# Loading the second weight matrix later, and accumulating the second matmul of the first two blocks and of the last quarter in one PSUM bank

## The chip, the cores and the metric

The kernel runs on one core of a Trainium2 chip. The metric is the device time of one execution in microseconds (us). Executions of the same kernel mostly spread over about 1 to 4 us here, so a difference of one microsecond needs several runs of both kernels on the same chip. Next to times I use profiles: one recorded execution per kernel, whose absolute times are exact for that execution but carry that execution's luck.

Engines are called as in the profile: PE is TensorE's matmuls and PEld its weight loads, DVE is VectorE, ACT is ScalarE, POOL is GpSimd, SP is SyncE. A "q" behind a name (POOLq) is the engine's instruction queue, which issues DMAs.

## The reference

```python
def _attn_ref(x, weight_gen):            # x (8, 4096, 192), weight_gen (8, 4096, 8, 7)
    w = softmax(weight_gen, axis=-1)     # 7 taps for each token and head
    # causal convolution over 7 tokens with these weights, 24 channels a head
    return einsum('bshk,bskhg->bshg', w, x_unf)   # ... unfolding cut

def _moe_ref(x, w_in, w_out):            # w_in (192, 2048), w_out (2048, 192)
    h = np.maximum(x @ w_in, 0.0)
    return h * h @ w_out
```

So 32,768 tokens go through a softmax, a convolution with weights that differ by token, and a feed-forward layer with a squared ReLU.

## The kernel before

All matmuls are in 16-bit floats. The tokens are worked off in blocks: two of 512 tokens, then 31 of 1024 (I call the first one block 0). For each block the softmax of the gate weights (`ex`, `ssum`, `rcp`, `v_first` or `v_big`) is written to bands: rows of it are read by DMA into `wr`, and VectorE multiplies them with a mask into band matrices `bd`. TensorE then does three kinds of matmul: the convolution (`yp`, line 393), the first matmul of the feed-forward layer (`h`, line 418) and the second (`o`, line 450). Between the last two, ScalarE evicts `h` with a ReLU into `t` and VectorE squares it into `g`.

The second matmul of a block is done during the next block, in passes (`M` in the schedule strings) of eight 128-row chunks and two 128-token columns. Before the change, each chunk is split into two 64-row halves that accumulate into two PSUM banks; ScalarE copies the first and VectorE adds the second:

```python
    def new_o(pool, tag):
        if pool is ps_o:
            return [ps_o.tile([P, TB], f32, name=f"o{i}") for i in range(2)]
        o = pool.tile([P, 2, TB], f32, name="o", tag=tag)
        return [o[:, 0], o[:, 1]]

    def st_mm2(j, qt, fcs, ccs, o):
        # ... half, off, per: cut
        for fc in fcs:
            g = g_t[(j, fc // per)][:, half, fc % per * th + off :]
            for cc in ccs:
                for oo, r0 in zip(o, (0, RT)):
                    nc.tensor.matmul(
                        out=oo[:, cc * Dm : (cc + 1) * Dm],
                        lhsT=g[r0 : r0 + RT, cc * P : (cc + 1) * P],
                        rhs=w_o[r0 : r0 + RT, fc, :],
                        start=(fc == 0 and cc == ccs[0]), stop=(fc == NF - 1),
                        skip_group_check=True,
                        tile_position=(r0, 0),
                    )

    def o_sum(j, qt, ccs, o):
        # ... cut
        nc.scalar.copy(out=o_sb, in_=o[0][:, c])
        nc.vector.tensor_tensor(out=o_sb, in0=o[1][:, c], in1=o_sb, op=AluOp.add)
```

The pool `ps_o` has one buffer for each of the two banks, so the next output's first matmul of a bank waits until that bank has been read: for the second bank, until VectorE's add.

The start of the kernel, which the change touches too, in the order in which the loads are issued:

```python
        spin(42)
        band_mask()
        s0.load(nc.sync)
        # ... w_in first half, first x, w_in second half, first softmax: cut
        x_load_f32(1)
        nc.scalar.copy(out=w_i[:, 1, 0], in_=w_st[1])
        cross_w_in(1)
        s1.load(nc.sync)
        # ... bands and convolution of block 0: cut
        x_cast(1, nc.vector.tensor_copy)

        nc.gpsimd.memset(x_t[0][:, 0, 0:1], 0.0)
        for q in (0, 1):
            load_w_out(q, 4)
        nc.gpsimd.memset(x_st[1][:, 0:1], 0.0)
        for q in (2, 3):
            load_w_out(q, 4)
        s2.load(nc.gpsimd)
        nc.gpsimd.memset(v_big, 0.0)
```

`s0`, `s1` and `s2` are the first three softmax parts; `s1.load` fetches the gate weights of the second. `spin(42)` is a warm-up of TensorE with matmuls on zeros. A `memset` on one element of a tile that something else still reads is a gate: GpSimd has to wait for that reader before it can go on to issue the loads behind it.

The softmax here doesn't subtract the row's maximum and nothing guards it: scores larger than these inputs give would overflow.

## Time and profile before

| | before |
|---|---|
| median of 3 runs | 753.37 us (753.17 to 754.48) |
| profiled span | 751.2 us |
| TensorE busy | 737.4 us, 98% |
| TensorE waits, 12 to 66 us | 8.0 us |
| after the last matmul | 3.66 us |

How to read this: an engine that is busy 98% of the span can only be helped where it is not busy. Busy shares of the other engines (VectorE and ScalarE 83% each) say that they can be the bound for a stretch, not overall. The lines that carry this stand in the prediction.

### The profile page before, as it was taken

What the parts mean: (1) busy time and instruction counts of PE and PEld (TensorE: products, weight loads), DVE (VectorE), ACT (ScalarE), POOL (GpSimd) and SP (SyncE); (2) the same over time, 40 slices, a digit from 0 to 9 for tenths busy, and PEclk for the clock granted to TensorE, in tenths of its full rate; (3) what the DMA queues carried; (4) which work ended last, traced back from release to release, by engine and by line L of the source; (5) the groups of instructions that cost most, each with busy time, mean ns of one, the idle gap of its engine ahead of it and who ended that gap; (6) DMA issues with size and microseconds to landing.
All of it is one profiled execution on the core that took longest, in us unless ns stands there. A gap on an engine that the chain in (4) does not pass through costs nothing.

```text
span 751.2 us, 33616 instructions
## 1 busy us (share of the span) xinstructions
PE 737.4 (98%) x15266; PEld 562.8 (75%) x15266; DVE 624.4 (83%) x1007; ACT 623.3 (83%) x753; POOL 88.0 (12%) x128
## 2 busy tenths in 40 slices
PE   8799999999999999999999999999999999999998
PEld 4667777777777787777877777787778777777787
DVE  5799999899789888888888888898888987777853
ACT  5787898888888888888888888888888888888883
POOL 4522221011101010011000110001100011001000
PEclk9999999999999999999999999999999999999999
DMA  8746443546443444533345442365341454441312
GB/s 222 130 80 126 68 76 91 114 94 139 72 87 97 85 79 79 116 92 63 57 80 139 82 81 51 55 138 107 59 73 51 59 108 79 59 74 50 50 45 65
DMA packets 122330, 65.22 MB, mean 87 GB/s; under 512 B 83881, under 2 KB 118668, under 8 KB 121676
## 3 DMA queue, kind: packets, MB, share of 16 engines
q1 hardware_dynamic: 77868, 46.05, 22.3%
q0 software_dynamic: 44176, 16.93, 20.4%
q8 instruction: 119, 1.95, 1.0%
q14 instruction: 23, 0.19, 0.1%
q10 hardware_dynamic: 144, 0.10, 0.0%
HBM read 48.61 MB, written 28.70 MB: 103 GB/s over the span
## 4 chain that ended last, share of the span: by engine, by line
PE 91%; DVE 4%; DMA 2%; SPq 1%; issue 1%; ACT 0%; POOL 0%; DVEq 0%; ACTq 0%
PE o L450 44%; PE h L418 42%; PE yp L393 6%; DVE g L430 1%; DMA wg<-in_weight_gen_dram 1%; DMA wr<-v_first 1%; DVE v_first L216 1%; DVE bd L325 1%; SPq L307 0%; DVE ssum L201 0%; DVE rcp L208 0%; SPq L125 0%; POOL wr L307 0%; DVE o_sb L465 0%; ACT ex L194 0%
## 5 line engine op out<-in xcount | busy, mean ns | idle before, releaser
L427 ACT ACTIVATE t<-h 128x1024 f16<-128x1024 f32 x512 | 497.2, 1027 | 66.0 <-PE h L418 64.9
L430 DVE TENSOR_TENSOR g<-t 128x1024 f16<-128x1024 f16 x512 | 334.4, 688 | 99.3 <-ACT t L427 96.3
L450 PEld LDWEIGHTS <-g 64*128 64x128 f16 x8192 | 351.7, 94 | 56.5 <-issue 3.7
L450 PE MATMUL o<-w_o,g 64*128 64x192 f16 x8192 | 384.0, 243 | 2.9 <-DVE o_sb L465 1.8
L418 PE MATMUL h<-y,w_i 64*128 64x512 f16 (+1 forms) x3168 | 377.7, 370 | 4.2 <-DMA w_i<-w_i 1.5
L418 PEld LDWEIGHTS <-w_i 64*128 64x128 f16 x3168 | 167.0, 94 | 112.9 <-issue 4.8
L325 DVE TENSOR_TENSOR bd<-wr,mask 128x4160 f16<-128x4160 f16 (+3 forms) x89 | 149.5, 1703 | 5.6 <-DMA wr<-v_first 5.6
L277 POOL DMA_DIRECT2D xt<-in_x_dram x62 | 51.3, 832 | 443.3 <-PE yp L393 420.4
L464 ACT COPY o_sb<-o 128x384 f32<-128x384 f32 x129 | 62.2, 482 | 34.0 <-PE o L450 34.0
L465 DVE TENSOR_TENSOR o_sb<-o,o_sb 128x384 f32<-128x384 f32 x129 | 71.2, 552 | 10.1 <-ACT o_sb L464 7.6
L404 ACT CAST y<-yp 128x1024 f16<-128x1024 f32 (+1 forms) x64 | 48.1, 802 | 16.4 <-PE yp L393 16.4
L393 PE MATMUL yp<-bd,xt 128*32 128x104 f16 (+8 forms) x3864 | 52.1, 208 | 1.8 <-DVE bd L325 1.6
L393 PEld LDWEIGHTS <-xt 128*32 128x32 f16 (+3 forms) x3864 | 46.2, 91 | 8.0 <-issue 7.4
L194 ACT ACTIVATE ex<-wg 128x448 f32<-128x448 f32 (+2 forms) x44 | 27.2, 619 | 3.6 <-DMA wg<-in_weight_gen_dram 3.6
L216 DVE TENSOR_TENSOR v_big<-ex,rcp 128x112 f16<-128x112 f32 (+1 forms) x136 | 27.4, 264 | 2.5 <-DMA vd<-v_big 1.3
L201 DVE TENSOR_REDUCE ssum<-ex 128x64 f32<-128x448 f32 (+2 forms) x44 | 26.1, 594 | 2.4 <-ACT ex L194 2.4
L208 DVE RECIPROCAL rcp<-ssum 128x64 f32<-128x64 f32 (+2 forms) x44 | 23.7, 539 | 1.5
L267 POOL DMA_DIRECT2D xt<-in_x_dram x7 | 3.8, 549 | 137.1 <-PE yp L393 137.1
L307 POOL DMA_DIRECT2D wr<-v_first x31 | 16.8, 562 | 21.3 <-DVE v_first L216 21.1
L512 PE MATMUL wp<-warm 128*128 128x512 f16 x42 | 10.8, 423 | 1.3 <-DVE warm L504 1.3
L512 PEld LDWEIGHTS <-warm 128*128 128x128 f16 x42 | 4.4, 108 | 7.1 <-issue 2.1
L216 DVE TENSOR_TENSOR v_first<-ex,rcp 128x112 f16<-128x112 f32 (+1 forms) x48 | 9.1, 256 | 0.3
(20 smaller groups left out, 24.6 us busy)
## 6 DMA issues: line engine op xcount, KB each, us to landing
out_dram<-o_sb SPq DMA_DIRECT2D x63, 384.0 KB, 2.9
xt<-in_x_dram POOLq DMA_DIRECT2D x42, 240.0 KB, 5.9
wg<-in_weight_gen_dram SPq DMA_DIRECT2D x4, 1064.0 KB, 8.4
xt<-in_x_dram POOLq DMA_DIRECT2D x20, 192.0 KB, 5.6
wr<-vd SPq DMA_DIRECT2D x38, 80.0 KB, 5.1
vd<-v_big SPq DMA_DIRECT2D x5, 512.0 KB, 5.6
wg<-in_weight_gen_dram SPq DMA_DIRECT2D x5, 392.0 KB, 5.2
wg<-in_weight_gen_dram SPq DMA_DIRECT2D x3, 616.0 KB, 5.8
```

Of the source, the lines that this page charges most:

```text
L194: nc.scalar.activation(out=self.ex[:, lo:hi].rearrange("p r g k e -> p (r g) k e"), in_=self.wg[:, lo:hi].rearrange("p r (g e) k -> p (r g ...
L216: eng.tensor_tensor(out=bass.AP(tensor=v.tensor, offset=v.offset + lo * H * SL + lo % SL * 2 + g * SL * 2, ap=[list(v.ap[0]), [H * SL + 2, ...
L277: eng.dma_start(out=dst[:, first:last], in_=ap)
L325: nc.vector.tensor_tensor(out=bd_t[j][:, H * lo : H * (lo + len(tiles) * n)].rearrange("p (g m c) -> p g m c", g=shape[1], c=2 * SL), in0= ...
L393: nc.tensor.matmul(out=yps[k // per][p0 : p0 + m, col + a : col + b], lhsT=x_t[s][:, i, 32 * q : 32 * q + m], rhs=bd[:, h // 2, h % 2, a - ...
L404: nc.scalar.copy(out=y[:, k0:k1, 0:th], in_=yp[:, 0 : (k1 - k0) * th].rearrange("p (k c) -> p k c", c=th),)
L418: nc.tensor.matmul(out=h[:, half, jj * th : (jj + 1) * th], lhsT=w_in_chunk(u * per + jj, slot, half), rhs=y_t[j][r0 : r0 + RT, k, 0:th], ...
L427: nc.scalar.activation(out=t1, in_=h, func=ActF.Relu)
L430: nc.vector.tensor_tensor(out=g, in0=t1, in1=t1, op=AluOp.mult)
L450: nc.tensor.matmul(out=oo[:, cc * Dm : (cc + 1) * Dm], lhsT=g[r0 : r0 + RT, cc * P : (cc + 1) * P], rhs=w_o[r0 : r0 + RT, fc, :], start=(f ...
L464: nc.scalar.copy(out=o_sb, in_=o[0][:, c])
L465: nc.vector.tensor_tensor(out=o_sb, in0=o[1][:, c], in1=o_sb, op=AluOp.add)
```

## The change

The intent has three parts. First, all of `w_out` is loaded behind the cast of the second x, so that the first half of it no longer shares the DMA engines with the second x, the second half of `w_in` and the gate weights of the second softmax. Second, in the first two blocks the second matmul uses all 128 rows of the array and one bank: no VectorE add and no wait for a second bank. Third, the last quarter of the last block does the same, so that the final store does not wait for an add. The diff, without blank-line hunks:

```diff
@@ -431,11 +432,11 @@
 
     QT = 2 * P
 
-    def new_o(pool, tag):
+    def new_o(pool, banks=2):
         if pool is ps_o:
-            return [ps_o.tile([P, TB], f32, name=f"o{i}") for i in range(2)]
-        o = pool.tile([P, 2, TB], f32, name="o", tag=tag)
-        return [o[:, 0], o[:, 1]]
+            return [ps_o.tile([P, TB], f32, name=f"o{i}") for i in range(banks)]
+        o = pool.tile([P, 2, TB], f32, name="o", tag="h")
+        return [o[:, i] for i in range(banks)]
 
     def st_mm2(j, qt, fcs, ccs, o):
 
@@ -446,11 +447,13 @@
         for fc in fcs:
             g = g_t[(j, fc // per)][:, half, fc % per * th + off :]
             for cc in ccs:
-                for oo, r0 in zip(o, (0, RT)):
+                n = P // len(o)
+                for i, oo in enumerate(o):
+                    r0 = n * i
                     nc.tensor.matmul(
                         out=oo[:, cc * Dm : (cc + 1) * Dm],
-                        lhsT=g[r0 : r0 + RT, cc * P : (cc + 1) * P],
-                        rhs=w_o[r0 : r0 + RT, fc, :],
+                        lhsT=g[r0 : r0 + n, cc * P : (cc + 1) * P],
+                        rhs=w_o[r0 : r0 + n, fc, :],
                         start=(fc == 0 and cc == ccs[0]), stop=(fc == NF - 1),
                         skip_group_check=True,
                         tile_position=(r0, 0),
@@ -462,7 +465,8 @@
         c = slice(ccs[0] * Dm, (ccs[-1] + 1) * Dm)
         o_sb = o_sb_t[(j, qt // 2)][:, qt % 2, c]
         nc.scalar.copy(out=o_sb, in_=o[0][:, c])
-        nc.vector.tensor_tensor(out=o_sb, in0=o[1][:, c], in1=o_sb, op=AluOp.add)
+        if len(o) == 2:
+            nc.vector.tensor_tensor(out=o_sb, in0=o[1][:, c], in1=o_sb, op=AluOp.add)
 
     def o_store(j, qt, chunks, eng):
 
@@ -543,11 +547,8 @@
         st_bands(1)
         x_cast(1, nc.vector.tensor_copy)
 
-        nc.gpsimd.memset(x_t[0][:, 0, 0:1], 0.0)
-        for q in (0, 1):
-            load_w_out(q, 4)
         nc.gpsimd.memset(x_st[1][:, 0:1], 0.0)
-        for q in (2, 3):
+        for q in range(4):
             load_w_out(q, 4)
         s2.load(nc.gpsimd)
         nc.gpsimd.memset(v_big, 0.0)
@@ -656,7 +657,7 @@
                     qt, part = divmod(m, 2)
                     m += 1
                     if part == 0:
-                        o = new_o(ps_o, None)
+                        o = new_o(ps_o, 1 if j < 3 else 2)
                     st_mm2(j - 1, qt, FCS[part], (0, 1), o)
                     if part == 1:
                         o_sum(j - 1, qt, (0, 1), o)
@@ -679,7 +680,7 @@
         j = NBLK - 1
         nq = 2 * BLOCKS[j][1]
         for qt in range(nq - 1):
-            o = new_o(ps_o if qt % 2 else ps_h, "h")
+            o = new_o(ps_o if qt % 2 else ps_h)
             st_mm2(j, qt, range(NF), (0, 1), o)
             o_sum(j, qt, (0, 1), o)
             if qt % 2:
@@ -687,7 +688,7 @@
             elif qt == nq - 2:
                 o_store(j, qt, (0, 1), nc.sync)
         for cc, eng in ((0, nc.sync), (1, nc.scalar)):
-            o = new_o((ps_h, ps_o)[cc], "h")
+            o = new_o((ps_h, ps_o)[cc], 1)
             st_mm2(j, nq - 1, range(NF), (cc,), o)
             o_sum(j, nq - 1, (cc,), o)
             o_store(j, nq - 2, (2 + cc,), eng)
```

New line numbers are 1 to 4 higher in the changed kernel: the convolution is L394, the first matmul L419, the second L453, the copy L467, the add L469, the exponential L195, the band product L326.

## The prediction

> **What bounds the kernel now.** I read the busy shares first, then the waits of the matmul engine by stretch of time, then the chain of waits and the timeline of the first 66 us, because the busy shares average stages with different limits.
>
> ```profile
> PE 737.4 (98%) x15266; PEld 562.8 (75%) x15266; DVE 624.4 (83%) x1007; ACT 623.3 (83%) x753; POOL 88.0 (12%) x128
> ```
>
> TensorE is busy for 98% of 751.2 us. Grouped by line between 62 and 747 us, its three kinds of matmul have together 0.1 us of idle time before them:
>
> ```profile
> L450 PE MATMUL o<-w_o,g 64*128 64x192 f16 x7909 | 370.0, 243 | 0.1
> L418 PE MATMUL h<-y,w_i 64*128 64x512 f16 x2880 | 353.6, 376 | 0.0
> L393 PE MATMUL yp<-bd,xt 128*32 128x104 f16 (+3 forms) x3480 | 45.9, 208 | 0.0
> ```
>
> So from 62 us on the time is pure TensorE work, and the change leaves that stretch alone until the last quarter. It can only win (a) TensorE idle time before 62 us, (b) what comes after the last matmul (747.6 us), and it can lose (c) if it makes a matmul pass dearer. The waits of TensorE from 12 to 66 us show what there is to win in (a): 8.2 us in six groups.
>
> ```profile
> PE o L450 <- DVE o_sb L465: 1.8, 2, 1.2
> PE yp L393 <- DVE bd L325: 1.6, 3, 1.1
> PE h L418 <- DMA w_i<-w_i: 1.5, 1, 1.5
> PE h L418 <- ACT t L427: 1.4, 2, 1.1
> PE h L418 <- ACT y L404: 0.9, 1, 0.9
> PE o L450 <- DVE g L430: 0.8, 1, 0.8
> ```
>
> Columns: who waited for whom, us in total, times, longest. The first row is the PSUM bank that VectorE has not yet added up; the third is the copy of w_in between partition halves that landed late; the others are mostly echoes of a late softmax. The chain of waits shows why it is late (start, us, what):
>
> ```profile
> 14.31 7.19 DMA wg<-in_weight_gen_dram
> ...
> 40.41 0.47 DVE o_sb L465
> ...
> 60.58 0.48 DVE o_sb L465
> ...
> 61.10 1.48 PE o L450 x31
> ```
>
> The gate weights of the second softmax take 7.19 us to land, at 21.50; those of the first took 3.18 us. ScalarE stands still for them (timeline, idle before in brackets):
>
> ```profile
> 21.60 0.94 ACT L194 ACTIVATE ex<-wg 128x784 f32<-128x784 f32 x1 [1.66 <-DMA wg<-in_weight_gen_dram]
> ```
>
> Everything up to 61 us hangs behind that exponential, through VectorE (sum, reciprocal, scaling, band products, squares). The DMA queues between 16.5 and 20.5 us say who is in the way:
>
> ```profile
> q0 software_dynamic: 917, 0.34, 74.8%
> q1 hardware_dynamic: 277, 0.64, 48.4%
> ```
>
> Columns: packets, MB, share of 16 engines (both together pass 100% because packets overlap). q0 here is nothing but the first quarters of w_out, issued from GpSimd at 13.43 and 14.21; q1 carries the second x, the second w_in copy and the gate weights. 0.34 MB of small packets take more engine time than 0.64 MB of what the engines are waiting for.
>
> **What the Trainium skill says.** "Trainium Kernel Development and Optimization", Key Constraints: DMAs of all queues run on the same 16 engines and interleave; the two shares above agree. "TensorE: Matmul & The Clock Gate", "Wait — 56ns, not 53.3ns?": a warm matmul of N columns costs N/2.4 + 2.5 ns, so 82.5 ns for 192 columns. The trace agrees for pairs of 64-row halves: a pass of 32 (16 pairs) takes 1.32 us of the chain, 82.5 ns a pair. The same page, "Back-to-back issue gap", gives 81 ns for a sustained weight-load-and-matmul of 128 columns, which I take as a hint that a weight load hides behind 80 ns of matmul but barely; no whole-array matmul of 192 columns stands in this trace (the warm-up's 512-column ones run at about 213 ns, weight loads hidden). "TensorEngine Tiling (Array Packing)", Key Properties: changing the tiling mode drains TensorE. The trace fits: from the last second-matmul start (57.03) to the first convolution matmul (57.20) is 0.17 us against 0.08 for a pair, so about 0.1 us a switch.
>
> **Part 1, w_out moved.** Nothing is removed; two of four loads (0.2 MB each as written) go behind the cast of the second x. From 16.5 to 21 us q1 moved about 0.67 MB at 48% of the engines or less. At the rate it had alone just before (about 0.17 MB per 0.5 us at 15.5), that is 2 us, so x lands near 17.1 instead of 17.7, the w_in copy near 18.0 instead of 19.99, and the gate weights near 18.9 instead of 21.50. The four w_out loads then are issued from about 17.9 at 0.75 us each; with about 2 us to the first packet they start near 19.8, after the gate weights.
> The gain is not 2.6 us, because ScalarE is busy with four first-matmul evictions until 19.95: the exponential moves from 21.60 to about 19.85, that is 1.75 us. TensorE's 1.48 us wait for the w_in copy (18.55 to 20.04) disappears too, but it is the same time: its next unit then waits for ScalarE behind that exponential. VectorE's sum and scaling, and the reads of the band rows, follow 1.75 us earlier.
> Does w_out come in time? First use moves from 24.84 to about 23.1, the second eight chunks from 26.8 to about 25.1. At 1.1 us a quarter (landings of the last two before: 22.87 and 23.89) I get 21.2, 22.3, 23.4, 24.4: in time by about 1 us each, and TensorE waits there for VectorE's squares anyway (0.76).
>
> **Part 2, one bank for blocks 0 and 1.** It removes four VectorE adds of 0.55 us, and the wait for the second bank. Two of the adds (at 30.34 and 47.50) stand before a wait for band rows (1.30 and 0.76 idle) and are worth nothing. The add at 40.33 is on the chain: 0.46. So VectorE is then 1.75 + 0.46 = 2.2 us early up to the squares that end at 60.58. The add at 60.49 is on the chain with the wait it causes: TensorE stood still 1.16 us before 61.10. The bank copied by ScalarE is free at 59.37, so this goes. Of it I give back 0.4: two passes later TensorE needs the square that VectorE does behind the softmax piece (at 62.94, ends 63.63; moved by 2.2 and the add's 0.48 it ends near 60.9), and TensorE would be there at about 60.6. The other wait for the bank (0.65 at 40.93) is in the shadow of the VectorE chain.
> Cost: matmuls halve (160 fewer instructions over the kernel, 16 instead of 32 a pass) but each pass still streams 16 times 192 columns, 1.32 us. Eight passes get up to two mode switches of 0.1 us each: at most 1.6 us of TensorE work before 58 us, nearly all inside waits. I charge 0.1.
>
> **Part 3, the last quarter.** The last two groups lose their 0.36 us adds:
>
> ```profile
> 747.54 0.32 ACT L464 COPY o_sb<-o 128x192 f32<-128x192 f32 x1 [0.93 <-PE o L450]
> 747.90 0.36 DVE L465 TENSOR_TENSOR o_sb<-o,o_sb 128x192 f32<-128x192 f32 x1 [0.89 <-ACT o_sb L464]
> 748.29 0.37 ACTq L470 DMA_DIRECT2D out_dram<-o_sb  x1
> ```
>
> The store can be issued when the copy ends, 747.88 instead of 748.29: 0.4. Against it stand one mode switch (0.1) and 32 whole-array matmuls; if their weight loads show by a few ns each, another 0.1 to 0.2. Net 0.15.
>
> **Sum.** 1.75 + 0.46 + 1.16 - 0.4 - 0.1 + 0.15 = 3.0 us, so 753.37 - 3.0 = 750.4 us, 0.4%.
>
> **Rivals.** (1) The w_out load becomes the new wait: issued 4 us later, it lands behind TensorE's need. For it: landings of 6.8 to 7.6 us in the crowded stretch before. Against it: 4.1 us for the later two, and the 1 us to spare worked out above. If w_out came 2 us later than I think, half of part 1 would go: 751.3.
> (2) Whole-array weight loads are not hidden. For it: weight loads take 94 ns each in the trace and a matmul of 192 columns only 80; side by side on two row halves they had twice the time. If a matmul then costs 110 ns, a pass costs 0.4 us more; the last quarter would lose 0.9 against 0.4 won, and the early passes would eat about 0.5: 752. Against it: in the same row half, matmuls with these loads already follow each other every 82 ns.
> (3) Everything before 61 us is bound by the reads of band rows and moves in their own rhythm (3.2 and 3.7 us on the chain), so early work only waits longer. Against it: those reads are issued by the scaling that part 1 moves. It would leave about 1.5 us of gain: 751.8.
> (4) More than I think: output stores, now issued when VectorE gets to its add (40.91), start after ScalarE's copy (37.40) and are out of the way of later reads. That might add 0.5 to 1: 749.5.
>
> **Range and chances.** My terms are each sure to a third or so, and the losses of (2) and (3) are likelier than (4): 749.1 to 752.2. Two per cent is 15 us; there are 8.2 us of TensorE waits and some 3.6 us of tail in all, and TensorE work is unchanged, so faster by over 2% cannot happen on this reading, and slower only if passes became several times dearer.
>
> **What would show it.** Right: gate weights landing in about 5 us instead of 7.19; the exponential near 19.9 after no wait, or one under 0.3; no TensorE wait for the w_in copy, none for VectorE's o_sb before 62 us; a small new wait for a square near 60 us; steady state from about 58 us; passes of blocks 0 and 1 of 1.3 to 1.5 us; last copy to last issue under 0.1 us. Wrong: a TensorE wait for w_out near 23 us; whole-array matmuls more than 90 ns apart; idle time before the band products longer than the 1.30 and 0.76 of before.

## The result, and the profile after

| | before | after |
|---|---|---|
| time, median of 6 runs each on the same chip | 753.92 us (752.67 to 754.91) | 751.69 us (749.92 to 752.74) |
| profiled span | 751.2 us | 749.2 us |

The ratio is 0.9968 with a 95% interval of 0.995 to 0.9985. A ratio is the mean time of one kernel's runs over that of the other's of the same rounds, so it is not quite the ratio of the medians. It amounts to 2.4 us less. The prediction was 750.4 (749.1 to 752.2).

The busy line of the changed kernel:

```profile
PE 739.0 (99%) x15106; PEld 559.8 (75%) x15106; DVE 621.8 (83%) x1001; ACT 623.0 (83%) x753; POOL 87.9 (12%) x127
```

There are 160 matmuls and 6 adds fewer, as planned, and TensorE is busy for 1.6 us more, not less: halving the number of matmuls removed no streaming. What went is idle time. TensorE's waits from 12 to 66 us (who waited for whom, us in total, times, longest):

```profile
PE yp L394 <- DMA xt<-in_x_dram: 1.2, 2, 1.1
PE h L419 <- ACT t L428: 0.9, 1, 0.9
PE h L419 <- ACT y L405: 0.9, 1, 0.9
PE o L453 <- DMA w_o<-in_moe_w_out_dram: 0.7, 1, 0.7
PE yp L394 <- DVE bd L326: 0.3, 1, 0.3
```

From 8.0 us in six groups to 4.0 us in five. The waits for the bank (`o_sb`), for `w_in` and for the square are gone in this profile. Two are new, both for a DMA: 0.7 for `w_out` and 1.2 for an x. Of the 4.0 us that TensorE no longer stands still at the start, only 2 arrive at the end. Part of the answer is in the groups between 62 and 746 us:

```profile
L453 PE MATMUL o<-w_o,g 64*128 64x192 f16 x7840 | 370.9, 243 | 0.9 <-issue 0.7
L419 PE MATMUL h<-y,w_i 64*128 64x512 f16 x2866 | 354.4, 376 | 0.0
L394 PE MATMUL yp<-bd,xt 128*32 128x104 f16 (+3 forms) x3480 | 46.0, 208 | 0.0
```

Busy time and mean durations are those of before; idle time before the second matmul is 0.9 us in place of 0.1, with nothing recorded that it waited for ("issue").

The second exponential on ScalarE, and the DMA queues from 16.5 to 20.5 us, both of the changed kernel:

```profile
19.97 0.96 ACT L195 ACTIVATE ex<-wg 128x784 f32<-128x784 f32 x1
```

```profile
q1 hardware_dynamic: 246, 0.56, 47.6%
q0 software_dynamic: 28, 0.01, 8.8%
```

In this profile part 1 looks just as predicted: `w_out` is out of the way (q0 74.8% before, 8.8% now), and the exponential starts 1.63 us earlier. The experiments show that this reading holds for this one profile and not for the kernel. The tail of the changed kernel:

```profile
745.88 0.32 ACT L467 COPY o_sb<-o 128x192 f32<-128x192 f32 x1 [1.00 <-PE o L453]
746.23 0.37 ACTq L474 DMA_DIRECT2D out_dram<-o_sb  x1
```

The last copy ends at 746.20 and the store is issued at 746.23; before, an add of 0.36 stood between.

I followed seven marks through both traces. The times are starts, except for the last two rows:

| mark (us) | before | after | after - before | step |
|---|---|---|---|---|
| second exponential | 21.60 | 19.97 | -1.63 | -1.63 |
| first wide band product (4160 columns) | 32.20 | 29.23 | -2.97 | -1.34 |
| sum of the third softmax | 40.79 | 37.35 | -3.44 | -0.47 |
| convolution for the fifth block | 81.53 | 78.41 | -3.12 | +0.32 |
| last convolution | 713.48 | 711.72 | -1.76 | +1.36 |
| end of the last matmul | 747.58 | 745.84 | -1.74 | +0.02 |
| span | 751.2 | 749.2 | -2.07 (unrounded) | -0.33 |

Three rows are not what I had predicted. The band product gains 1.34 us on top of what comes from before it, where I had foreseen nothing. The fifth block's convolution loses 0.32 us, where I had 0.76 of gain from the bank (1.16 less 0.4). And 1.36 us are lost between 81 and 713 us, where I had said that the change touches nothing.

### The profile page after: what moved, and what is told of

Same layout as the page of the kernel before. It is cut to its first block, busy times and chain, and to the rows that moved or that the text cites. A ratio compares the mean times of both kernels' runs of the same rounds, so it can differ in the third digit from the quotient of the medians.

```text
span 749.2 us, 33282 instructions
## 1 busy us (share of the span) xinstructions
PE 739.0 (99%) x15106; PEld 559.8 (75%) x15106; DVE 621.8 (83%) x1001; ACT 623.0 (83%) x753; POOL 87.9 (12%) x127
## 4 chain that ended last, share of the span: by engine, by line
PE 88%; DVE 5%; DMA 3%; ACT 1%; issue 1%; SPq 0%; POOL 0%; DVEq 0%; ACTq 0%
PE o L453 42%; PE h L419 40%; PE yp L394 6%; DVE g L431 2%; DVE bd L326 1%; DMA xt<-in_x_dram 1%; ACT t L428 1%; DMA x_st<-in_x_dram 1%; DMA vd<-v_big 1%; DVE v_first L217 1%; DVE ssum L202 0%; DVE rcp L209 0%; DMA wg<-in_weight_gen_dram 0%; DVE o_sb L469 0%; POOL wr L308 0%
## 5 line engine op out<-in xcount | busy, mean ns | idle before, releaser
L453 PEld LDWEIGHTS <-g 64*128 64x128 f16 (+1 forms) x8032 | 353.0, 94 | 55.7 <-issue 5.0
L453 PE MATMUL o<-w_o,g 64*128 64x192 f16 (+1 forms) x8032 | 386.1, 243 | 1.7 <-DMA w_o<-in_moe_w_out_dram 0.7
L419 PE MATMUL h<-y,w_i 64*128 64x512 f16 (+1 forms) x3168 | 379.8, 370 | 2.1 <-ACT t L428 0.9
L419 PEld LDWEIGHTS <-w_i 64*128 64x128 f16 x3168 | 165.5, 94 | 114.7 <-issue 5.0
L326 DVE TENSOR_TENSOR bd<-wr,mask 128x4160 f16<-128x4160 f16 (+3 forms) x89 | 149.4, 1702 | 4.6 <-DMA wr<-v_first 4.6
L467 ACT COPY o_sb<-o 128x384 f32<-128x384 f32 x129 | 62.3, 483 | 33.2 <-PE o L453 33.2
L469 DVE TENSOR_TENSOR o_sb<-o,o_sb 128x384 f32<-128x384 f32 x123 | 68.2, 554 | 8.0 <-ACT o_sb L467 5.6
L405 ACT CAST y<-yp 128x1024 f16<-128x1024 f32 (+1 forms) x64 | 48.2, 803 | 16.5 <-PE yp L394 16.5
L394 PE MATMUL yp<-bd,xt 128*32 128x104 f16 (+8 forms) x3864 | 52.0, 208 | 1.8 <-DMA xt<-in_x_dram 1.2
L394 PEld LDWEIGHTS <-xt 128*32 128x32 f16 (+3 forms) x3864 | 46.1, 91 | 8.0 <-issue 6.4
L195 ACT ACTIVATE ex<-wg 128x448 f32<-128x448 f32 (+2 forms) x44 | 27.2, 618 | 1.9 <-DMA wg<-in_weight_gen_dram 1.9
```

Of the source, the lines that this page charges most:

```text
L195: nc.scalar.activation(out=self.ex[:, lo:hi].rearrange("p r g k e -> p (r g) k e"), in_=self.wg[:, lo:hi].rearrange("p r (g e) k -> p (r g ...
L326: nc.vector.tensor_tensor(out=bd_t[j][:, H * lo : H * (lo + len(tiles) * n)].rearrange("p (g m c) -> p g m c", g=shape[1], c=2 * SL), in0= ...
L394: nc.tensor.matmul(out=yps[k // per][p0 : p0 + m, col + a : col + b], lhsT=x_t[s][:, i, 32 * q : 32 * q + m], rhs=bd[:, h // 2, h % 2, a - ...
L405: nc.scalar.copy(out=y[:, k0:k1, 0:th], in_=yp[:, 0 : (k1 - k0) * th].rearrange("p (k c) -> p k c", c=th),)
L419: nc.tensor.matmul(out=h[:, half, jj * th : (jj + 1) * th], lhsT=w_in_chunk(u * per + jj, slot, half), rhs=y_t[j][r0 : r0 + RT, k, 0:th], ...
L453: nc.tensor.matmul(out=oo[:, cc * Dm : (cc + 1) * Dm], lhsT=g[r0 : r0 + n, cc * P : (cc + 1) * P], rhs=w_o[r0 : r0 + n, fc, :], start=(fc ...
```

## The experiments

**My theory after the result.** (T1) The early gain is real: w_out's move, the missing add and the bank. (T2) The extra 1.34 us at the band product come from the reads of the band rows meeting something else on the DMA engines. (T3) The loss after 81 us is chance stops of TensorE. **Rivals:** the move of `w_out` gives nothing and something else moved the exponential; the loss after 81 us is caused by the changed schedule; whole-array passes cost time of their own.

All kernels below gave correct results. The three groups shared runs of the kernel before: 754.70 us median of 11 runs for `e4_all`, `e1_wout`, `e2_bank`, `e3_tail`; 753.11 of 9 for `e9_phase`, `e10_phase`, `e8_dummy`, `e5_whole`; 754.17 of 11 for `e11_nomove`, `e6_gate`, `e12_gates_first`, `e7_early_x`. The times in one table ("us less" is 1 minus the ratio, times the median of before; negative is slower):

| run | median us (range) | ratio to before, 95% | us less |
|---|---|---|---|
| e4_all | 752.11 (750.56 to 754.14) | 0.9969 (0.9951 to 0.9986) | 2.3 |
| e1_wout | 753.83 | 0.9990 (0.9975 to 1.0005) | 0.8 |
| e2_bank | 752.05 | 0.9964 (0.9948 to 0.9981) | 2.7 |
| e3_tail | 753.73 | 0.9988 (0.9974 to 1.0002) | 0.9 |
| e9_phase | 752.28 (751.89 to 753.23) | 0.9988 (0.9975 to 1.0001) | 0.9 |
| e10_phase | 752.23 (750.82 to 752.47) | 0.9985 (0.9971 to 0.9999) | 1.1 |
| e8_dummy | 751.80 (750.90 to 754.34) | 0.9985 (0.9965 to 1.0005) | 1.1 |
| e5_whole | 798.40 | 1.0598 (1.0577 to 1.0620) | -45.0 |
| e11_nomove | 753.61 (749.58 to 755.22) | 0.9989 (0.9969 to 1.0009) | 0.8 |
| e6_gate | 752.70 (750.90 to 754.11) | 0.9978 (0.9962 to 0.9993) | 1.7 |
| e12_gates_first | 751.42 (750.19 to 752.93) | 0.9967 (0.9952 to 0.9982) | 2.5 |
| e7_early_x | 750.42 (750.10 to 750.92) | 0.9952 (0.9940 to 0.9965) | 3.6 |

The intervals are 1 to 1.5 us to each side, so the times alone cannot rank the parts. The verdicts below come from the marks in the traces wherever there is one.

One thing disturbs both. In seven of the 14 profiles (e4_all, e1_wout, e2_bank, e3_tail, e9_phase, e8_dummy and e11_nomove) TensorE's granted clock was at half for 3.4 us, beginning somewhere between 15.9 and 22.3 us; e11_nomove has a second such window. The first profiles of the kernel before and of the changed kernel have none. It shows in the mean granted clock of a run: of the 11 runs of the kernel before in the first group, the three at 1.0 took 753.0 to 753.9 us and the eight below it 754.0 to 756.9.

### The changed kernel once more: e4_all

No edit; the changed kernel as it is, run again.

> The changed kernel again, unaltered, for a second profile and a second set of times. My theory: the change gains about 3.2 us before 64 us of the span (in the first profile the first fully busy matmul stretch starts 3.2 us earlier), nothing at the end, and the first profile lost 1.4 us of it between 66 and 712 us to short stops of TensorE without a recorded wait, which fall at random. So here: time 2 to 3.3 us under the kernel before, the convolutions of blocks 5 to 9 again 3.1 us earlier (within 0.3), and a different sum and different places of the short stops. Rival: the stops belong to the change; then the same places (near 194 and 353 us) lose about 0.5 us each again.

It took 2.3 us less, as at first (2.4). But its profile is not the first one: the second exponential starts at 21.40, not at 19.97, and the fifth block's convolution at 79.61, not at 78.41. So the 1.63 us of part 1 in the first profile do not belong to the kernel. TensorE's wait of 1.5 us for the second copy of `w_in`, gone in the first profile, is back as well.

The semaphore updates of the gate-weight load in the trace say what happens. A DMA's landing is 16 updates, one for each engine. In the first profile of the changed kernel, the eighth comes at 18.89 and the last at 19.55. In this one the eleventh comes at 19.03, the fifteenth at 20.34 and the last at 21.30. The Trainium skill, "DMA: Bandwidth & Descriptors", "Why a DMA increments its semaphore by 16 and not by 1", says that a DMA runs on up to 16 engines that finish independently, and only the full 16 means that the data are there. The trace agrees: ScalarE starts 0.1 us after the sixteenth in e4_all (in the first profile 0.4, when it has finished the eviction before).

As for the stops of TensorE after 81 us: there were again some of 0.3 to 0.5 us with no recorded wait, at 127.9, 196.0, 355.7, 490.9 and 625.6 us, 634.43 us in all from the fifth convolution to the last, against 633.31 in the first profile and 631.95 before. Two of the places are those of the first profile, 194.3 and 353.7: counted in matmuls from the start they are the same. Chance alone is therefore not a good account of them; what they are is told in the section on why the prediction was right or wrong. This is one of the first profile's stops:

```profile
193.55 0.41 PE L453 MATMUL o<-w_o,g 64*128 64x192 f16 x5
...
194.28 0.92 PE L453 MATMUL o<-w_o,g 64*128 64x192 f16 x18 [0.32 <-issue]
```

A pass breaks off after 5 of its matmuls and goes on 0.3 us later; the bracket names no releaser.

### The move of w_out alone: e1_wout

```diff
-        nc.gpsimd.memset(x_t[0][:, 0, 0:1], 0.0)
-        for q in (0, 1):
-            load_w_out(q, 4)
         nc.gpsimd.memset(x_st[1][:, 0:1], 0.0)
-        for q in (2, 3):
+        for q in range(4):
             load_w_out(q, 4)
```

> Only the w_out loads moved, two banks everywhere. My theory: the exponential of the second softmax starts near 20.0 us instead of 21.6, ScalarE-bound, and this is passed on: TensorE is fully busy 1.2 to 1.7 us earlier, time 1.2 to 1.7 us under the kernel before. There is a wait for w_out of 0.5 to 1 us near 23 to 24 us that costs nothing. Rival: the landing of x for blocks 2 and 3 (36.6 us in the changed kernel) takes the place of the softmax, and less than 0.8 us are left.

The queues from 16.5 to 20.5 us, and ScalarE's second exponential, both in this run:

```profile
q1 hardware_dynamic: 228, 0.52, 48.8%
q8 instruction: 1, 0.02, 2.0%
```

```profile
21.71 0.95 ACT L194 ACTIVATE ex<-wg 128x784 f32<-128x784 f32 x1
```

No packet of `w_out` is there any more (no q0), and the exponential starts at 21.71 against 21.60 before. Two things hold it up. One is the landing: twelve of the 16 engines were done by 19.10 and fifteen by 19.70, against eight by 20.69 and fifteen by 21.28 before. So the move does what it was meant to do on fifteen engines, some 1.6 us. The sixteenth came at 21.26 and took it all back. The other is ScalarE: the eviction before the exponential ends at 21.83 instead of 19.95, in a profile whose TensorE was at half clock from 15.9 to 19.3 us. So the exponential would not have started earlier here with a punctual sixteenth engine, and between runs the landings are the better mark. In the window stands one packet of q8, 16 KB of instructions; it started at 18.14 and occupies one engine (its 1.27 us there are the 2.0% of its line). In the first profile of the changed kernel the corresponding packet started at 15.29, before the gate weights were under way. That this packet makes the slow engine fits in time in both, but nothing here isolates it for this load, and e10_phase is a doubtful case: its packet started at 14.36, yet its last engine is 1.2 us behind the fifteenth. The time, 0.8 us less with an interval that includes no difference, does not contradict the trace.

### One bank in the first two blocks alone: e2_bank

```diff
-                        o = new_o(ps_o, None)
+                        o = new_o(ps_o, 1 if j < 3 else 2)
...
-            o = new_o((ps_h, ps_o)[cc], "h")
+            o = new_o((ps_h, ps_o)[cc])
```

(with the changed `new_o`, `st_mm2` and `o_sum`; `w_out` is loaded as before, the last quarter is as before.)

> Only the one bank for blocks 0 and 1, w_out as before, last quarter as before. My theory: the waits for the second bank (0.65 and 1.16 us) and 0.46 us of VectorE on the chain go, less 0.4 for a square: 1.2 us, more if the wait for the square does not come (1.6). Rival: the bank's wait was an echo of a late VectorE, and below 0.5 us are gained.

2.7 us less, the largest of the three parts taken alone. Its marks: the exponential at 21.55, as before; the wide band product at 30.77 instead of 32.20; the band product to the sum of the third softmax in 8.12 instead of 8.59; the fourth convolution to the fifth in 22.91 instead of 24.33. So the extra 1.4 us at the band product, which I could not place, come with this part, although `w_out` stands where it stood. That ruled out my first guess that the reads of the band rows are faster because `w_out` is out of their way.

### The last quarter alone: e3_tail

```diff
-            o = new_o((ps_h, ps_o)[cc], "h")
+            o = new_o((ps_h, ps_o)[cc], 1)
```

(with `new_o(ps_o, 2)` in all passes before.)

> Only the last quarter on the whole array. My theory: 0.4 us less between the last copy and the last store, 0.1 us more of matmul time for one switch of mode: 0.2 to 0.3 us faster, below what five rounds resolve, so read from the profile: last matmul to the end of the span 0.4 us shorter, matmuls of the last block 0.1 us longer. Rival: whole-array matmuls are dearer, the last 32 take 0.5 us more and the time is the same or longer.

From the last matmul's end to the end of the span: 3.32 us (3.66 before, 3.33 in the changed kernel). The last block's own work takes 10.90 us, against 10.80 before and in `e1_wout`: the whole-array matmuls give 0.10 back. Net 0.23 us. The measured 0.9 us less has an interval from -0.15 to 2.0 and does not add to that.

### Instruction fetches and the reads of the band rows: e9_phase and e10_phase

In the page of the profile, queue q8 carries 119 packets of 16 KB before, 118 after. TensorE has 2 x 15266 instructions before and 2 x 15106 after (matmuls and weight loads); divided by 256, this is 119.3 and 118.0. So q8 is TensorE's instruction fetch, one packet for 256 instructions. The Trainium skill, "Runtime: NRT & Kernel Launch", "Instruction fetch mechanics", says the same of the 16 KiB blocks of 256 instructions, and that the cost of crossing a block is "mostly hidden". For TensorE itself that is so at most of these places, though not at all of them, as will be seen. But the packet lies on one of the 16 DMA engines, and takes 0.9 to 1.35 us there in nine of ten cases in these traces. Before, the third fetch starts at 29.80, 2.34 us after the first read of the band rows is issued, and of the fifth read fifteen engines are through by 30.83 while the last comes at 32.18.

If that is the cause, TensorE's instruction count alone must move it. One bank saves 64 instructions up to there (two passes of 16 matmuls and 16 weight loads fewer). So I changed only the warm-up, to the same number of columns in other portions: 84 x 256 = 21504 columns instead of 42 x 512 in the kernel before, and 74 x 292 = 21608 in the changed one, which brings back the 64 instructions that one bank had saved.

```diff
 # e9_phase, from the kernel before; e10_phase, from the changed one, has 0:292 and spin(74)
-                    out=wp[:, 0:TB], lhsT=warm[:, 0:P], rhs=warm, start=True, stop=True
+                    out=wp[:, 0:256], lhsT=warm[:, 0:P], rhs=warm[:, 0:256], start=True, stop=True
...
-        spin(42)
+        spin(84)
```

> The kernel before, with the 42 warm-up matmuls of 512 columns made 84 of 256: the same columns, 84 instructions more at the start, so each 16 KB fetch of TensorE instructions comes 84 instructions earlier in the work. My theory: in the kernels with two banks the third fetch (29.4 to 29.9 us, 2.3 us after the first read of band rows) takes about 1 us of one of the 16 DMA engines, and the fifth band-row read lands 1.2 to 1.4 us late behind it; here the fetch comes near 27, before those reads move, so the time from the end of the second scaling to the first wide band product falls from 4.5 to 4.8 us to about 3.4, and the matmuls are steady about 1.2 us earlier, as in the one-bank kernels. Rival: one bank itself (VectorE's missing add, ScalarE's earlier copy) makes the reads land sooner; then that time stays at 4.5 or more.

> The changed kernel with 74 warm-up matmuls of 292 columns in place of 42 of 512: 64 instructions more, as many as the first two passes of one bank save, so the third fetch falls where it fell before. My theory: it comes about 2.3 us after the first band-row read again, the fifth read lands about 1.2 us late, scaling to band product 4.5 us in place of 3.4 to 4.1, time 0.7 to 1.3 us over the changed kernel, so 1.2 to 1.9 under the kernel before. Rival (one bank itself does it): stays at 3.4 to 4.1 and the time stays 2.4 under the kernel before.

VectorE from the scaling that issues the reads to the band product that waits for them, in the kernel before:

```profile
25.97 1.46 DVE L216 TENSOR_TENSOR v_first<-ex,rcp 128x112 f16<-128x112 f32 x8
...
32.20 2.33 DVE L325 TENSOR_TENSOR bd<-wr,mask 128x4160 f16<-128x4160 f16 x1 [1.30 <-DMA wr<-v_first]
```

and in e9_phase:

```profile
26.13 1.46 DVE L216 TENSOR_TENSOR v_first<-ex,rcp 128x112 f16<-128x112 f32 x8
...
31.00 2.33 DVE L325 TENSOR_TENSOR bd<-wr,mask 128x4160 f16<-128x4160 f16 x1
```

From the end of the one to the start of the other, 4.77 us became 3.41, and VectorE's wait of 1.30 is gone; the work that stands between is the same. The DMA queues from 29.5 to 31.0 us before, with the fetch in the middle of the reads:

```profile
q1 hardware_dynamic: 414, 0.05, 20.9%
q0 software_dynamic: 89, 0.04, 15.1%
q8 instruction: 1, 0.02, 5.0%
```

In e9_phase the third fetch starts at 27.13, before the first read is issued at 27.62, and the same window has no packet of q8.

The reverse, e10_phase, starts the fetch 1.88 us after the first read of the changed kernel, instead of 3.67, and the same stretch takes 4.47 us in place of 3.41. In that run three engines were late with leftovers of `w_out` and of the third gate weights as well, so only e9_phase is a clean case. Over these profiles the stretch takes 4.5 to 4.8 us where the fetch starts 1.9 to 2.4 us after the first read (before, e1_wout, e3_tail, e10_phase), and 3.4 to 4.1 where it comes earlier (e9_phase) or 3.3 to 3.8 us after it (after, e4_all, e2_bank). The six kernels that follow below, all with one bank, fit: the fetch comes 3.2 to 4.0 us after the first read, and the stretch takes 3.3 to 3.7 us, in e8_dummy too, where VectorE has its adds back. I take the cause as shown: part 2 gained about 1.3 us at the band product by shortening TensorE's program by 64 instructions, which let a fetch slip past the reads. A different warm-up would have bought it as well: e9_phase took 0.9 us less than before, though that interval just includes no difference. How much of the 1.3 us reaches the end is not shown: in e10_phase, where the reads are slow again, the fifth block's convolution starts at 78.81, in the middle of the kernels with one bank (78.25 to 80.42, e5_whole and e11_nomove left out).

### The add without its bank: e8_dummy

```diff
             nc.vector.tensor_tensor(out=o_sb, in0=o[1][:, c], in1=o_sb, op=AluOp.add)
+        elif len(ccs) == 2:
+            nc.vector.tensor_tensor(out=spare, in0=spare, in1=spare, op=AluOp.add)
```

(from the changed kernel; `spare` is a zeroed tile of 128 x 384.) VectorE does the work of the removed adds, but nobody waits for a second bank.

> The changed kernel with a spare VectorE add of the same shape (in SBUF, waiting for nothing, not holding the bank) in place of each of the four adds that one bank saves. My theory: of those only the one at the end of the second pass group is on the chain, so the time from the first wide band product to the sum of the third softmax grows from 8.1 to about 8.6 us (8.59 with the real add), TensorE does not wait for a bank, and the time is 0.5 to 1 us over the changed kernel (two of the four adds matter). Rival: all four adds count, 2.2 us lost; or none.

The idle add of e8_dummy stands before the sum of the third softmax, as the real one did before:

```profile
39.40 0.55 DVE L471 TENSOR_TENSOR spare<-spare 128x384 f32<-128x384 f32 x1
39.87 0.61 DVE L202 TENSOR_REDUCE ssum<-ex 128x64 f32<-128x448 f32 x1
```

In the changed kernel the sum follows the square at once:

```profile
35.55 1.89 DVE L431 TENSOR_TENSOR g<-t 128x1024 f16<-128x1024 f16 x3
37.35 0.61 DVE L202 TENSOR_REDUCE ssum<-ex 128x64 f32<-128x448 f32 x1
```

From the wide band product to that sum: 8.59 in all four kernels that have the add and in e8_dummy, 8.12 in the changed kernel and e2_bank, 8.13 in e4_all. So the add is worth 0.47 on VectorE's chain. From the fourth convolution to the fifth: 24.33 before, 23.36 in e8_dummy, 22.90 in the changed kernel.

What makes the difference there are waits for a bank. Before, TensorE stood still for 1.16 us at 61.10 (and 0.28 for a ReLU just ahead of it), together the 1.43 us that the changed kernel saves. In e8_dummy that wait is gone, but a smaller one appears three passes later, at the next output that has two banks again, since the idle add has made VectorE late:

```profile
65.29 1.48 PE L453 MATMUL o<-w_o,g 64*128 64x192 f16 x31 [0.35 <-DVE o_sb L469]
```

And in e9_phase, which has two banks and every add but an earlier VectorE, the wait of 1.16 is less than half as long:

```profile
59.26 1.48 PE L450 MATMUL o<-w_o,g 64*128 64x192 f16 x31 [0.52 <-DVE o_sb L465]
```

So the second bank does not cost a fixed 1.16 us. It costs by how much VectorE is behind TensorE when the pass begins, and the same microsecond can be won by the bank or by an earlier VectorE, but not twice.

### One bank everywhere: e5_whole

```diff
-                        o = new_o(ps_o, 1 if j < 3 else 2)
+                        o = new_o(ps_o, 1)
```

> The second matmul of all blocks but the last on the whole array into one bank. My theory: a pass costs 0.1 us more for each switch of mode, two a pass, some 120 further passes, so 20 to 25 us slower (2.7 to 3.3%), with matmuls inside a pass 82 ns apart as in pairs. Rival 1: weight loads show, matmuls 95 to 110 ns apart, 45 us or more slower. Rival 2: switches are free and the missing adds of VectorE help, no difference.

It took 45 us more than before; I had expected about half, because I had counted 120 further passes. There are 240: e5_whole has 3840 matmuls fewer than the changed kernel, 16 a pass. The last matmul ends at 793.38 instead of 745.84, so 47.54 / 240 = 0.198 us a pass, two mode switches of 0.1 us. The steady state of e5_whole, first matmul, pass, first matmul:

```profile
204.07 0.82 PE L419 MATMUL h<-y,w_i 64*128 64x512 f16 x6
204.82 1.49 PE L453 MATMUL o<-w_o,g 128*128 128x192 f16 x16
206.25 0.82 PE L419 MATMUL h<-y,w_i 64*128 64x512 f16 x6
```

and of the kernel before:

```profile
201.93 1.48 PE L450 MATMUL o<-w_o,g 64*128 64x192 f16 x32
203.25 0.81 PE L418 MATMUL h<-y,w_i 64*128 64x512 f16 x6
203.90 1.48 PE L450 MATMUL o<-w_o,g 64*128 64x192 f16 x32
```

Start to start, the pass takes 1.43 instead of 1.32, and the six matmuls before a pass 0.75 instead of 0.65: 0.1 at each edge. Inside the pass the whole-array matmuls follow each other every 82 to 83 ns (the first one 92 to 93), so the weight loads stay hidden. This settles rival (2) of the prediction: it is the switch that costs, not the weight load. It also shows why the change stops after two blocks.

### Everything but the move: e11_nomove

```diff
+        nc.gpsimd.memset(x_t[0][:, 0, 0:1], 0.0)
+        for q in (0, 1):
+            load_w_out(q, 4)
         nc.gpsimd.memset(x_st[1][:, 0:1], 0.0)
-        for q in range(4):
+        for q in (2, 3):
             load_w_out(q, 4)
```

(from the changed kernel.)

> The changed kernel with the w_out loads put back where they were (one bank and whole-array last quarter stay). My theory: moving w_out brings 14 of 16 DMA engines home 1.5 us earlier but not the slowest one, so the exponential moves by 0.2 us at most in most runs, and w_out itself, and the third gate weights behind it, land later; without the move the kernel is as fast as the changed one within 0.5 us, 2 to 3 us under the kernel before. Rival (the prediction): it loses 1 us or more against the changed kernel.

0.8 us less than before, in an interval from -0.7 to 2.3, with that of e8_dummy the widest of all: this run is inconclusive. Its profile fell on an unlucky start: TensorE's granted clock was at half in two windows (16.2 to 19.6 and 40.0 to 43.5 us), and the fifth block's convolution starts at 82.68, later than before. Its first stretch agrees with the rest (band rows 3.42). Set against e2_bank, which differs only by the tail and took 2.7 us less, it shows how far apart two runs of nearly one kernel can lie.

### Another gate for w_out: e6_gate

```diff
-        nc.gpsimd.memset(x_st[1][:, 0:1], 0.0)
+        nc.gpsimd.memset(wr_t[1][:, 0, 0, 0:1], 0.0)
```

(from the changed kernel: the loads wait for the band product of block 1 rather than for the cast of the second x.)

> The changed kernel with the w_out loads held back by the band products of the second block (16.9 us) in place of the cast of the second x (18.2 us). My theory: w_out lands 1.3 us earlier and TensorE's wait for it (0.6 to 0.7) goes, but the wait was off the chain: same time within 0.5 us. Rival: 0.7 us faster than the changed kernel.

TensorE's wait of 0.7 for `w_out` is gone, and the time is 1.7 us less than before, no better than the changed kernel's 2.3 and 2.4; the fifth block's convolution starts at 78.25, against 78.41 in the changed kernel's first profile. So the wait was beside the path that sets the end, as far as an interval from 0.5 to 2.9 us can tell.

### The gate weights before the second x: e12_gates_first

```diff
         x_cast(0, nc.scalar.copy)
+        s1.load(nc.sync)
         x_load_f32(1)
         nc.scalar.copy(out=w_i[:, 1, 0], in_=w_st[1])
         cross_w_in(1)
-        s1.load(nc.sync)
```

(from the changed kernel.)

> The changed kernel with the load of the second gate weights put ahead of the load of the second x on the same queue. My theory: the gate weights land near 16 instead of 19.5 to 21.7, the exponential starts when ScalarE is free (20.0 to 20.3) in every run, and the matmuls are steady 0.8 to 1.5 us earlier than in most profiles of the changed kernel: 0.5 to 1.2 us faster than it, 3 to 3.6 under the kernel before. Rival: x and the second w_in copy, now behind them, land about 1 us later and take the place of the gate weights; no gain.

The gate weights land at 16.27, earlier than in any other run, but the exponential starts at 20.26, since ScalarE is busy until then, and the second copy of `w_in` between partition halves now lands at 21.29. TensorE waits 2.2 us in two pieces for copies of `w_in`, more than for anything else from 12 to 66 us.

One late load has been traded for another; the 2.5 us less are the changed kernel's.

### The x of the third block issued earlier: e7_early_x

The chain that ended last in the changed kernel has a new long piece, 7.83 us from 28.78 for loads of x, and TensorE's timeline shows where it ends:

```profile
36.65 1.58 PE L394 MATMUL yp<-bd,xt 128*32 128x104 f16 x118 [1.05 <-DMA xt<-in_x_dram]
```

The loads of x for the next block (parts 2 and 3 of x) are issued from GpSimd between 28.78 and 30.22, and the last lands at 36.60; before, TensorE came late enough not to notice. So I issued them ahead of the third gate weights, with the gate of e6_gate:

```diff
-        nc.gpsimd.memset(x_st[1][:, 0:1], 0.0)
+        nc.gpsimd.memset(wr_t[1][:, 0, 0, 0:1], 0.0)
         for q in range(4):
             load_w_out(q, 4)
+        x_load(2)
+        x_load(3)
         s2.load(nc.gpsimd)
...
-            if j == 0:
-                x_load(2)
-                x_load(3)
-            elif j < NBLK - 2:
+            if 0 < j < NBLK - 2:
```

> As e6_gate, with the loads of x for blocks 2 and 3 issued before the third gate weights in place of behind the band-row reads. My theory: TensorE's wait for x before the third convolution (0.5 to 1.1 us) goes, but the band-row reads of GpSimd queue behind x and land later by up to 1.5 us, and VectorE waits for them: no gain or up to 0.7 us slower than the changed kernel. Rival: the wait for x is on the chain and up to 1 us is gained.

The same convolution in e7_early_x:

```profile
36.54 1.61 PE L394 MATMUL yp<-bd,xt 128*32 128x104 f16 x120
```

x lands at 27.95 and the convolution waits for nothing, so the rival of my expectation held. At 750.42 us this is the fastest kernel, 3.6 us less than before (2.6 to 4.5), and its runs spread by only 0.8 us. On the same chip e6_gate, which differs by the place of these loads alone, took 752.70 (750.90 to 754.11). Part of what its profile shows is the removed wait: its exponential started at 21.42, 1.45 later than in the changed kernel's first profile, and yet its fifth convolution starts at 78.33 against 78.41. Another part is that it had hardly any stops later: 632.11 us to the last convolution, against 633.31 and 634.43. Those stops stand where TensorE waits for instructions (next section), and in this profile few of the fetches came late. Whether the edit causes that, I cannot say.

## Why the prediction was right or wrong

The time (751.69) lies in the range (749.1 to 752.2), and the sum, 3.0 us, was 0.6 us too large. Its terms were less right than its sum: a term that was far too large and a gain that had no term nearly made up for each other, which was luck. (Two small slips without effect: the rows of waits that it sums to 8.2 us make 8.0, and the later two quarters of `w_out` took 4.1 and 4.4 us, not 4.1 both.)

**Part 1, 1.75 us: mis-sized.** The step that failed is "the gate weights near 18.9 instead of 21.50", worked out from total bytes and engine shares. It is right for most of the 16 engines (1.6 us earlier for the fifteenth in e1_wout) and wrong for the landing, which is the last of the 16. Over the profiles that were compared, the second exponential starts at 21.30 on average with the move (six: after, e4, e1, e10, e8, e5) and at 21.66 without it (five: before, e2, e3, e9, e11): 0.36 us in place of 1.75. The landings, which do not depend on ScalarE, give about the same: 21.09 and 21.50 on average, 0.41 apart, while the fifteenth engine is 1.3 us earlier (19.90 and 21.23). In the first profile of the changed kernel it was 1.63, and the prediction would have looked confirmed if that profile had been all. That an instruction fetch makes the last engine late here is argued from its times, not shown.

**w_out in time: wrong, without effect.** I had the four quarters at 21.2, 22.3, 23.4 and 24.4; they came at 24.09, 24.50, 25.69 and 26.75. The issue was at 18.75, not 17.9, and their packets came in bulk only from 21.0. So rival (1) did occur as a wait (0.7 us) but cost nothing that e6_gate could recover.

**The add on the chain, 0.46: right.** 0.47 measured, with e8_dummy as the counter-proof.

**The bank, 1.16, less 0.4 for a wait for the square: the first right for this schedule, the second too careful.** The stretch from the fourth to the fifth convolution shrank by 1.43: the 1.16 and, with it, the 0.28 of the ReLU wait. In kernels with two banks whose VectorE was early anyway the wait was 0.52 (e9_phase) and 0.64 (e1_wout), so the term is right only as one of the ways in which these microseconds can be won. The feared wait did not come, because the fourth block's band product was 2.65 us earlier in the changed kernel while its convolution was only 1.70 us earlier: VectorE had gained more than TensorE, and its squares were ready.

**That same gap is the first give-back.** VectorE's earlier work could not all be used, because between the third and the fourth convolution TensorE and ScalarE's evictions set the pace. From the fourth block's band product to its convolution went 6.64 us before and 7.38 to 7.59 wherever the band product was early by 0.95 us or more, with two banks too (7.38 in e9_phase, 7.48 in e1_wout). The prediction had VectorE's gain arriving in full.

**What was missing: the fetch between the reads, 1.3 us.** Rival (3) said that the reads of the band rows keep their own rhythm. They do not: they took 1.3 to 1.4 us less, and e9_phase shows that the place of one instruction fetch decides it. I had no term for this; at the band product it made good most of what part 1 lacked.

**"From 62 us on the time is pure TensorE work, and the change leaves that stretch alone": right for the work, wrong for the time.** Between the fifth convolution and the last, the changed kernel needed 1.36 us more in its first profile and 2.48 us more in e4_all, in stops of 0.1 to 0.5 us that no recorded wait explains. Counting the matmuls tells what they are. Between 66 and 747 us the 14 profiles hold 28 idle times of TensorE over 60 ns without a recorded wait. All 28 stand before matmul number 128 n + 96 for a whole n: one place in every 256 TensorE instructions, the length of a fetched block. The block before was in each case mostly convolution (93 or more of its 128 matmuls), whose matmuls are short: TensorE went through it in 2.3 to 3.7 us, where the other blocks took 7.3 us (median). And in each case TensorE goes on 1.2 to 1.6 us after the end of the last fetch packet; at the other 1487 such places it never comes earlier than 1.2 us after its packet. So these stops are waits for instructions. They account for the loss: they cost 0.28 us before, 1.39 in the first profile and 2.42 in e4_all, and without them the stretch takes 631.5 to 631.9 us in all 13 kernels but e5_whole (my estimate, from how far each profile falls behind the others at these places).

My theory of chance and its rival were both half right. The places are fixed, and the change leaves them where they were, since blocks 0 and 1 lose 128 matmuls and 128 weight loads, just one block of 256. Which of them cost time differs from one execution to the next. Kernels with the old schedule in this stretch lose time there too (0.63 us in e1_wout, 0.76 in e3_tail, 1.38 in e9_phase, whose warm-up shifts the places), and e7_early_x, with the new one, only 0.28. Whether the changed kernel's fetches are late more often stays open.

**Mode switches, 0.1, and the tail, 0.15: right.** A switch costs 0.1 us (e5_whole), the tail gains 0.33 and pays 0.10, so 0.23.

**The parts do not add up.** Taken alone they gave 0.8, 2.7 and 0.9 us less, 4.4 in all; together 2.3 and 2.4. With intervals of 1 to 1.5 us this need not mean anything. The traces offer reasons why they should not add: an earlier VectorE and the missing bank remove the same wait, and an earlier start of VectorE is cut off by the pace of TensorE and ScalarE. How much of the 2.4 us the move of `w_out` contributes can't be settled from these runs: by e4_all against e2_bank it is nothing, by e11_nomove (0.8 us less, on another chip and with a wide interval) up to 1.5.

## What to carry to other kernels

A load lands when the slowest of the 16 DMA engines is through, so estimate a landing from the last engine's queue, and check more than one profile before you credit a removed transfer with a faster one. When an early stretch becomes faster, look at which transfer was issued just in time until now: here issuing the next x earlier (e7_early_x) took 3.6 us off, where the same kernel without it (e6_gate) had 1.7 and the changed kernel 2.4. Expect part of a gain on a helper engine to be cut off where the bound engine sets the pace. And when a busy engine stops without a recorded wait, count its instructions up to the stop: if the counts agree modulo the length of a fetched block, it probably waits for instructions.

## What the Trainium skill lacked or had wrong

- "Runtime: NRT & Kernel Launch", "Instruction fetch mechanics" calls the fetch mostly hidden. It lacks that the fetch packet of 16 KB sits 0.9 to 1.35 us on one of the 16 DMA engines and delays loads that use it: 4.77 us against 3.41 from scaling to band product, with the same work (before, e9_phase). It also lacks when the fetch is not hidden: TensorE stopped at 28 of 1515 block ends, all behind a block that it had gone through in 2.3 to 3.7 us, and went on 1.2 to 1.6 us after the packet's end; this cost the changed kernel 1.4 and 2.4 us in two profiles.
- "TensorEngine Tiling (Array Packing)", "Key Properties" says that a mode switch drains TensorE but gives no cost: 0.1 us a switch, 0.198 us for a pass with two (e5_whole, 240 passes).
- "TensorE: Matmul & The Clock Gate", "Back-to-back issue gap" gives some 131 ns for sustained pairs of weight load and matmul at 512 columns. The warm-up's pairs follow each other every 216 ns here, and whole-array pairs of 192 columns every 82 to 83 ns; both agree with the formula N/2.4 + 2.5 that the page offers for the isolated case.
- "DMA: Bandwidth & Descriptors" explains the 16 updates but not how far apart they can be: 1.5 us between the fifteenth and the last in e1_wout, for a load of 392 KB.
